# One more slot between a spectrum job's products and its way back, in a kernel of attention and a long convolution

## Chip, core and metric

The kernel runs on one core of one Trainium2 chip. The metric is the device time of one execution in microseconds (us), the median of several runs. Beside the runs there is one execution that the hardware profiler recorded; all rows of a trace come from that one.

## What is computed

Two independent layers over 2048 positions and 448 channels, float32, put side by side in the output:

```python
def _A_ref(u, log_A_real, A_imag, C_real, C_imag, log_dt, D_skip):   # a state-space convolution
    dt = jnp.exp(log_dt)
    A = -jnp.exp(log_A_real) + 1j * A_imag
    C = (C_real + 1j * C_imag) * dt[:, None]
    P = jnp.exp((A * dt[:, None])[:, :, None] * pos[None, None, :])
    K = 2.0 * jnp.einsum("dn,dnl->dl", C, P).real
    Kf, Uf = jnp.fft.rfft(K, 2 * L), jnp.fft.rfft(u_t, 2 * L)
    y = jnp.fft.irfft(Uf * Kf[None], 2 * L)[:, :, :L]
    return y + u * D_skip                                            # (transposed back)
def _B_ref(x, wqkv, wo):                                             # attention, 16 heads of 28
    q, k, v = split_heads(x @ wqkv)
    p = softmax(q @ k.T * Dh ** -0.5)
    return merge_heads(p @ v) @ wo
out = concatenate([_A_ref(...), _B_ref(...)], axis=-1)
```

## The kernel before

**The attention sets the rhythm.** After a stage of projections the kernel runs 256 steps (`NS`, line 32): 16 units `u` (4 groups of 4 heads times 4 blocks of 512 queries), with 16 blocks of 128 keys each. A step `s` does, for the current unit, four score matmuls into `pss`, each followed by an exponential on ScalarE (`s_mm`, line 714), and for the step before the four products of probabilities and values into `po` (`pv_step`, line 721, eight matmul records of 128x512). It also does, for the unit after, four matmuls into `pm` whose maxima VectorE takes (`max_mm`); these run 19 steps ahead, so they end at step 236, and the steps from 237 on are shorter. Within a step the order is written out by hand:

```python
ORDER = ('m0', 's0', 'm1', 's1', 'v', 'f', 'pv', 'f', 'v', 'k', 'm2', 's2', 'm3', 's3', 'v')
FX, PD, GAP = 1, 2, 2
```

All engines keep this program order in the stage.

**Slots.** Each `'f'` is a slot: `slot(s_)` (line 957) counts it in `n_slot` and runs at most one small task of other work, the first that is ready in this list: urgent tasks of the attention (the sums of the exponentials and the scaling of a finished unit, `fin`, line 734; the transposed maxima), an output projection (`project`, line 760), kernel powers and the input's transform, and then the convolution's spectra (kind "s"), and when none of these can run, its finish jobs (kind "f"). A step has two slots, one ahead of the `po` matmuls and one behind them; from step 238 on (`late`) a third one follows at the step's end. Behind the last step a loop calls `slot` until nothing is left.

**Spectra.** From step 195 on, 16 jobs (2 halves `f` of the channels, 8 blocks each) multiply the two transforms (`spectrum`, line 776). A job has four tasks: `forth(0)`: 16 matmul records `pm<-yk,mw`, and two VectorE products `pr` with the input's transform `ub`; `last`: `forth(1)`, the same for the other part, and then `join(0)` and `join(1)`, two GpSimd (POOL) instructions each, which make `p0` and `p1` of the products; `back(0)`: 16 matmul records `pm<-p,mw` that read `p0`, a copy `y` on ScalarE and a DMA to `z`; `back(1)`: the same from `p1`. In front of each task stands the number of slots that it must stay behind the task before it:

```python
return load, [(0, lambda: forth(0)), (0, last), (GAP, lambda: back(0)), (0, lambda: back(1))], None
```

and `f_slot` (line 929) tests it, in slots and not in time:

```python
gap, t = f_tasks[kind][0]
if n_slot[0] < f_next[kind] + gap:
    return False
```

Where a spectrum task has to wait, the slot goes to a finish job if one is ready, and stays empty otherwise. The tiles `pr` and `p` have one buffer, and the loads of the next job's `yk`, `mw` and `ub` are issued when a job's first task is taken up.

**Finish jobs.** For each half, once its 8 spectra are done (`s_done`, line 915), four jobs (`finish`, line 819) load `zi` (896 KB, from the `z` of all eight spectra) and the input `ut`, scale `ut` on GpSimd, and run four tasks of 8 matmul records `pm<-zi,wb` with an addition on VectorE into `ot` and, every second time, two DMAs to the output. A finish job starts at the earliest three steps after its load (`FL`).

All DMAs are issued in order on the SP queue. Every row of the trace bears line 75 (L75), where a helper records the instructions, so rows are told apart by their tiles.

Of the kernel before, what the change touches and what calls it, by code (L numbers as in the profile page):

```python
# [33 lines left out]
ORDER = ('m0', 's0', 'm1', 's1', 'v', 'f', 'pv', 'f', 'v', 'k', 'm2', 's2', 'm3', 's3', 'v')  # L34
PB = 8
F1 = 2
FX, PD, GAP = 1, 2, 2
FL = {"s": 2, "f": 3}
S0, SP, SW, SD, PW, E3 = 0, 4, 0, 5, 37, 8
UG = (2, 2, 4)  # L40
# [1089 lines left out]
```

## Time and profile before

| | |
|---|---|
| median of 3 runs | 1319.46 us (1316.6 to 1322.87) |
| the profiled execution | 1316.79 us, of which its instructions span 1315.1 |
| mean granted TensorE clock | 0.98 |
| busy in the span | TensorE 94%, VectorE 72%, ScalarE 72%, GpSimd 66% |

A row of the timeline has the start and the duration in us, engine, operation, the tile written and the tiles read, the shape, and how many instructions were merged; in brackets the idle time of the engine ahead of it and what ended it. PE is TensorE, DVE VectorE, ACT ScalarE, POOL GpSimd, SPq a DMA issued from SP. A row of the windows has the length of the stretch, the busy time of each engine with its count, the granted clock, the DMA share and GB/s. A row of the waits has who waited for whom, the total in us, the number of times and the longest.

### The profile page before, as it was taken

How to read it: one execution, taken by the hardware profiler on the slowest of the kernel's cores; microseconds unless marked ns; L12 is line 12 of the kernel's file. 1: busy time of each engine (PE TensorE's matmuls, PEld its weight loads, DVE VectorE, ACT ScalarE, POOL GpSimd, SP SyncE). 2: the span in 40 equal slices, each digit the busy share in tenths (PEclk: the TensorE clock that was granted, in tenths of full speed). 3: DMA queues.
4: the chain of work that ended last, by engine and by line, in shares of the span. 5: the costliest groups of instructions: out<-in, count | busy, mean ns of one | idle time of the engine just before them, and what ended most of it. 6: DMA issues, size and time to landing. Idle time of an engine off the chain costs nothing.

```text
span 1315.1 us, 33199 instructions
## 1 busy us (share of the span) xinstructions
PE 1229.7 (94%) x12625; PEld 698.8 (53%) x12625; DVE 948.6 (72%) x2106; ACT 953.0 (72%) x2068; POOL 870.4 (66%) x736
## 2 busy tenths in 40 slices
PE   6879985899999999999999999999999899999897
PEld 4657763455555555555555555555555444544333
DVE  5898887878777777778778888888887545645111
ACT  4876762488888888888788888888887656646453
POOL 3686681398887788887779999989993414423311
PEclk9989987899999999999999999999999999999999
DMA  6677769736765546468633233732416553925485
GB/s 190 206 276 260 242 205 285 220 73 143 179 147 132 129 136 175 131 174 224 167 100 87 61 78 90 161 80 70 101 37 175 178 158 132 284 87 186 132 219 137
DMA packets 200087, 205.35 MB, mean 156 GB/s; under 512 B 95992, under 2 KB 158520, under 8 KB 197880
## 3 DMA queue, kind: packets, MB, share of 16 engines
q1 hardware_dynamic: 199928, 203.23, 55.9%
q8 instruction: 100, 1.64, 0.5%
q14 instruction: 59, 0.48, 0.1%
HBM read 120.73 MB, written 82.18 MB: 154 GB/s over the span
## 4 chain that ended last, share of the span: by engine, by line
PE 71%; DVE 9%; POOL 7%; DMA 5%; ACT 4%; issue 4%; SPq 0%; ACTq 0%; POOLq 0%; DVEq 0%
PE pm L75 40%; PE pss L75 16%; PE po L75 15%; POOL p L75 2%; DMA k<-hl 2%; DVE tri L75 2%; POOL e L75 1%; DVE mx L75 1%; POOL qhat L75 1%; DVE sg L75 1%; ACT tri L75 1%; DVE px L75 1%; DVE qhat L75 1%; DMA khat<-k 1%; ACT p L75 1%
## 5 line engine op out<-in xcount | busy, mean ns | idle before, releaser
L75 ACT ACTIVATE p<-pss 128x512 f32<-128x512 f32 x1024 | 560.9, 610 | 112.3 <-PE pss L75 109.1
L75 DVE TENSOR_REDUCE mx<-pm 128x1 f32<-128x512 f32 x500 | 321.7, 684 | 125.5 <-PE pm L75 123.4
L75 PE MATMUL pss<-qhat,khat 128*128 128x512 f32 x1024 | 403.3, 400 | 2.3 <-ACT p L75 2.3
L75 PE MATMUL pm<-khat,qhat 128*128 128x512 f32 x749 | 327.1, 440 | 3.4 <-DVE mx L75 2.3
L75 POOL TENSOR_TENSOR e<-e,sdb 128x256 f32<-128x256 f32 x168 | 202.1, 1203 | 118.4 <-ACT e L75 63.1
L75 PE MATMUL po<-p,v 128*32 128x512 f32 x2048 | 269.8, 595 | 0.0
L75 POOL TENSOR_TENSOR e<-e,eu 128x256 f32<-128x256 f32 x168 | 248.3, 1478 | 13.2
L75 PEld LDWEIGHTS pm<-khat,qhat 128*128 128x128 f32 x749 | 141.9, 190 | 197.3 <-ACT p L75 41.9
L75 DVE CUSTOM_DVE_ANT_0 rl<-pm,rl 128x512 f32<-128x512 f32 x249 | 171.5, 689 | 64.8 <-ACT rl L75 61.8
L75 PEld LDWEIGHTS pss<-qhat,khat 128*128 128x128 f32 x1024 | 191.1, 189 | 49.0 <-issue 12.2
L75 POOL TENSOR_TENSOR eu<-e,sdb 128x256 f32<-128x256 f32 x168 | 202.3, 1204 | 0.0
L75 POOL TENSOR_TENSOR p<-pr,pr 64x448 f32<-64x448 f32 x64 | 73.0, 1141 | 149.6 <-PE pm L75 128.6
L75 ACT ACTIVATE rl<-pm 128x512 f32<-128x512 f32 x249 | 150.8, 606 | 20.9 <-PE pm L75 20.9
L75 DVE TENSOR_TENSOR g<-g,zg 128x128 f32<-128x128 f32 x392 | 162.1, 414 | 3.4
L75 PE MATMUL pm<-xh,khat 112*128 112x512 f32 x256 | 90.6, 436 | 21.8 <-DVE hl L75 10.5
L75 PE MATMUL pm<-kdif,qhat 128*128 128x512 f32 x249 | 101.3, 407 | 2.4 <-DMA v<-v 1.3
L75 DVE TENSOR_TENSOR zg<-g,zg 128x128 f32<-128x128 f32 x224 | 87.9, 393 | 5.0
L75 PEld LDWEIGHTS pm<-e,g 128*32 128x32 f32 x3584 | 57.2, 109 | 43.8 <-issue 17.0
L75 ACT ACTIVATE y<-pm 128x448 f32<-128x448 f32 x48 | 26.4, 549 | 73.1 <-PE pm L75 37.7
L75 PE MATMUL pm<-e,g 128*32 128x64 f32 x3584 | 73.1, 222 | 1.9 <-POOL e L75 1.9
L75 PEld LDWEIGHTS pm<-xh,khat 112*128 112x128 f32 x256 | 52.0, 208 | 37.8 <-DVE hl L75 12.9
L75 ACT ACTIVATE ub<-pm 128x224 f32<-128x224 f32 (+1 forms) x96 | 38.8, 449 | 40.0 <-PE pm L75 38.1
(134 smaller groups left out, 1468.7 us busy)
## 6 DMA issues: line engine op xcount, KB each, us to landing
sdb<-sd SPq DMA_DIRECT2D x56, 336.0 KB
khat<-k SPq DMA_DIRECT2D x64, 256.0 KB
qhat<-q SPq DMA_DIRECT2D x64, 256.0 KB
sd<-sg SPq DMA_DIRECT2D x8, 1456.0 KB
k<-hl SPq DMA_DIRECT2D x16, 512.0 KB
q<-hl SPq DMA_DIRECT2D x16, 512.0 KB
mw<-in_mw SPq DMA_DIRECT2D x16, 512.0 KB
sd<-qhat SPq DMA_DIRECT2D x8, 896.0 KB
```

The source lines that it names most:

```text
L75: i = f(*args, **kw)
```

## The change

`GAP` is 3 in place of 2: `back(0)` of a spectrum job may be issued in the third slot behind `last` at the earliest, and not in the second. Nothing else is edited. Each step is still built by the same functions, so the tasks of the spectra and the finish jobs shift against the attention's matmuls: the first job keeps its slots, the fifteen others move, the last `back(1)` stands in step 247 in place of 241, and the first finish job of the second half starts in step 250 in place of 249. Of the tasks of the finish jobs, three more run behind the last step.

```diff
-FX, PD, GAP = 1, 2, 2
+FX, PD, GAP = 1, 2, 3
```

## The prediction

> **What bounds the kernel now.** I read the page's engine line first, then busy time by stage, the waits of the stage that runs the spectra, and TensorE's timeline there.
>
> ```profile
> PE 1229.7 (94%) x12625; PEld 698.8 (53%) x12625; DVE 948.6 (72%) x2106; ACT 953.0 (72%) x2068; POOL 870.4 (66%) x736
> 900.00:950.00 50.00, 49.81 (x610) 28.40 (x610) 43.62 (x106) 42.34 (x97) 46.07 (x37) 1.00 0.34 83
> 1000.00:1050.00 50.00, 45.82 (x492) 24.82 (x492) 29.73 (x63) 31.20 (x63) 18.24 (x16) 1.00 0.51 167
> PE pm L75 <- POOL p L75: 14.4, 18, 2.0
> ```
>
> TensorE sets the pace (94%). Before the spectra (900 to 950, columns PE, PEld, DVE, ACT, POOL, clock, DMA) it stands at 49.81 of 50 us; once they run it falls to 45.82, while VectorE and ScalarE have 20 us to spare and POOL 30. So nobody else is the limit: TensorE waits, and the last row (taken over 990 to 1265) says for whom: 18 times for POOL's tile `p`, the input of the way back. One job in TensorE's timeline, with its VectorE and POOL work:
>
> ```profile
> 1092.46 0.39 PE L75 MATMUL pss<-qhat,khat 128*128 128x512 f32 x1
> 1092.78 0.96 PE L75 MATMUL pm<-p,mw 128*32 128x224 f32 x16
> 1093.56 1.04 PE L75 MATMUL po<-p,v 128*32 128x512 f32 x8
> 1094.42 0.94 PE L75 MATMUL pm<-yk,mw 128*32 128x224 f32 x16
> ...
> 1097.41 0.96 PE L75 MATMUL pm<-yk,mw 128*32 128x224 f32 x16
> 1098.19 1.04 PE L75 MATMUL po<-p,v 128*32 128x512 f32 x8
> 1099.16 0.50 PE L75 MATMUL pm<-khat,qhat 128*128 128x512 f32 x1
> ...
> 1100.89 0.39 PE L75 MATMUL pss<-qhat,khat 128*128 128x512 f32 x1
> 1102.16 0.96 PE L75 MATMUL pm<-p,mw 128*32 128x224 f32 x16 [0.88 <-POOL p L75]
> 1102.94 1.04 PE L75 MATMUL po<-p,v 128*32 128x512 f32 x8
> 1104.59 0.96 PE L75 MATMUL pm<-p,mw 128*32 128x224 f32 x16 [0.61 <-POOL p L75]
> 1098.44 1.16 DVE L75 TENSOR_TENSOR pr<-pm,ub 128x448 f32<-128x448 f32 x2
> 1099.77 4.76 POOL L75 TENSOR_TENSOR p<-pr,pr 64x448 f32<-64x448 f32 x4 [9.63 <-PE pm L75]
> ```
>
> `yk,mw` is a forth, `p,mw` a back. The second forth (in `last`) starts at 1097.41; its products end 1099.60, then POOL's four joins take 4.76 us. back(0) needs the first two of them and starts at 1102.16, 4.75 us after the forth; back(1) needs all and starts at 1104.59, 7.18 after it. These two distances are the job's own latency, and the change does not alter them. GAP 2 puts back(0) one step behind the forth, at 1100.89 + 0.32 = 1101.21 if it could, hence the wait. (A slot follows a `pss` at 0.32 us, 1092.46 to 1092.78, and a `po` at 0.86, 1093.56 to 1094.42; the bracketed idle counts from the modelled end of the matmul, 0.39 and 1.04, so it understates the delay by 0.07 or 0.18.)
>
> **What the change removes.** The row of waits holds 14.4 us in 18; with 0.13 each for the modelled ends that is 16.7. One more is hidden by a half clock:
>
> ```profile
> 1214.61 0.94 PE L75 MATMUL pm<-yk,mw 128*32 128x224 f32 x16
> 1219.30 0.96 PE L75 MATMUL pm<-p,mw 128*32 128x224 f32 x16 [1.92 <-POOL p L75]
> 1220.08 1.75 PE L75 MATMUL po<-p,v 128*32 128x512 f32 x8
> 1221.73 1.72 PE L75 MATMUL pm<-p,mw 128*32 128x224 f32 x16
> 1218.00:1221.00 3.00, 1.70 (x24) 0.68 (x24) 0.00 (x0) 0.82 (x2) 2.79 (x4) 0.88 1.07 370
> 1221.00:1224.00 3.00, 3.00 (x22) 1.02 (x18) 0.00 (x0) 0.44 (x1) 0.67 (x1) 0.55 1.05 244
> ```
>
> The back(1) at 1221.73 comes 2.43 us after its back(0), where 0.78 + 0.86 = 1.64 would do: 0.8 more. Together 17.5 us. Behind the 1.92 us wait the granted clock falls to 0.55; the 16 matmuls take 1.72 instead of 0.96 us, and with the `pss` behind them some 0.9 us are lost, which go with the wait. [...]
>
> **What is left of the waits.** I followed the slot function, and the built order of both programs, job by job. Of the 16 jobs, job 0 keeps its slots. Where the forth lies in the slot behind `pv`, or an urgent task, projection or finish task stands between, the third slot puts back(0) over 5 us behind it and back(1) in a later step: no wait (jobs 2, 3, 4, 7 to 11, 13, 14). Where the forth lies in the slot ahead of `pv` and the slots between are empty (jobs 1, 5, 6), back(0) now comes behind the next step's `pv`: 0.78 (1097.41 to 1098.19) + 0.97 (to 1099.16) + 2.05 (to 1101.21) + 0.86 = 4.66 us, against 4.75: 0.1 each, 0.3 in all; back(1) is then half a step later and free.
>
> Jobs 12 and 15 fall into the steps without maximum matmuls, which are short:
>
> ```profile
> 1270.22 0.59 PE L75 MATMUL pm<-zi,wb 128*32 128x224 f32 x8
> 1270.63 1.04 PE L75 MATMUL po<-p,v 128*32 128x512 f32 x8
> 1271.49 0.56 PE L75 MATMUL pm<-zi,wb 128*32 128x224 f32 x8
> 1271.98 0.73 PE L75 MATMUL pss<-qhat,khat 128*128 128x512 f32 x2
> 1272.64 0.59 PE L75 MATMUL pm<-zi,wb 128*32 128x224 f32 x8
> 1273.82 0.59 PE L75 MATMUL pm<-zi,wb 128*32 128x224 f32 x8
> 1276.43 0.49 PE L75 MATMUL pss<-qhat,khat 128*128 128x512 f32 x1 [0.29 <-ACT p L75]
> 1279.58 0.59 PE L75 MATMUL pm<-zi,wb 128*32 128x224 f32 x8
> ```
>
> Three filled slots make a step of 3.60 us (1270.22 to 1273.82): three finish tasks of 0.41, 0.49 and 0.52, a `pv` of 0.86 and two pairs of `pss` of 0.66. With a forth (0.78 or 0.87) in place of one finish task, three slots span 3.95 us: back(0) waits 0.8. Then back(1) is one slot on, 0.87 + 0.66 or 0.78 + 0.86 us, against 2.43: 0.85. Both jobs: 3.3. So 3.6 us of waits stay, and 17.5 - 3.6 = 13.9 go. Bounds: 17.5 if none stays, 10.3 if twice as much stays as I count.
>
> **What moves.** The work itself is the same instructions. The job that ended in step 241 ends in 247, and a few finish tasks (`zi,wb`) move later. In a step whose two later slots are empty, TensorE waits for an exponential (0.29, row 1276.43): two of them, 1273.82 to 1279.58 with one task of 0.41, take 5.76 us, 2.68 each without the task, where a filled one takes 3.60 less its three tasks, 2.18. So such a step wastes 0.5 us. Before, seven steps of these are so (245, 247, 248, 250, 251, 253, 254), after it five (249, 251, 252, 254, 255): 1.0 gained. Three finish tasks more run behind the last step:
>
> ```profile
> 1295.63 1.08 PE L75 MATMUL pm<-ident,rb 128*32 128x128 f32 x32 [1.05 <-ACT rb L75]
> 1288.93 0.59 PE L75 MATMUL pm<-zi,wb 128*32 128x224 f32 x8
> ```
>
> One of them fills part of the 1.05 us wait for `rb`: 0.4 gained. The others cost no more there than in a step.
>
> **What it adds.** The second half's finish jobs need every block `z` of that half. Before, the last back was six steps ahead of the first such load; now the load stands one slot behind it, as it does for the first half in the trace of before:
>
> ```profile
> 1116.83 0.96 PE L75 MATMUL pm<-p,mw 128*32 128x224 f32 x16
> 1118.62 0.37 SPq L75 DMA_DIRECT2D z<-y  x1
> 1121.12 0.57 SPq L75 DMA_DIRECT2D zi<-z  x1
> 1259.78 0.40 SPq L75 DMA_DIRECT2D zi<-z  x1
> 1260.28 1.34 SPq L75 DMA_DIRECT2D ut<-in_A_u  x2
> 1267.48 2.11 POOL L75 TENSOR_TENSOR ut<-ut,dsk 128x896 f32<-128x896 f32 x1 [10.38 <-DMA ut<-in_A_u]
> ```
>
> From the back (1116.83) to the load's issue (1121.12) are 4.3 us, on SP behind the `z` write; only the finish job's own loads and outputs queue behind it there. A load with its `ut` behind it has landed at most 7.7 us later (1259.78 to 1267.48), so `zi` is there between 4.3 and 12.0 us after the back. Its first matmul stands in step 250; by the slot costs above it comes 0.87 + 0.66 + 0.52 + 0.66 (rest of step 247), 3.6 (248), 2.65 (249) = 9.0 us after the back. So TensorE waits 0 to 3.0 us. `ut` was issued later and landed last, so `zi` is well below its bound: I take 0.5. [...]
>
> **Sum.** 13.9 + 0.9 + 1.0 + 0.4 - 0.5 = 15.7 us off the profiled execution's 1316.79 (span 1315.1 and 1.7 around it): 1301.1. That execution is 2.7 below the median of 1319.46, so for a median I say 1303.8, which is 1.2% less.
>
> **Rivals.**
> Another engine takes over the wait. In the stage VectorE holds the products and maxima, and could hold TensorE where POOL did; half of the 15.7 would remain: 1311.6. Against it: 29.73 of 50 us busy, and 43.62 beside a TensorE at 49.81.
> The `z` load is late: 3.0 us of wait instead of 0.5, and a half clock behind it at the 0.9 it cost above: 1303.8 + 3.4 = 1307.2. For it: a write and a read that depends on it now stand in a row. [...] Against: `zi` has `ut` behind it in the 7.7 us.
> Slower: the finish transfers become the chain that ends last. From the last back the new order leaves about 51 us to the end (9.0; two rounds of three steps, 3.60 + 5.76 each; and 23.5 from the third of the half's finish jobs on: it started at 1288.93, 26.2 before the end, and now has one filled step of 3.6 less and two tasks more behind it); the four remaining loads at 7.7 us in a row, 4.3 ahead of them and some 9 behind make 44. At twice the 7.7 they make 75, 24 us past the end: 1328. It decides from about 9.4 us a load on, and eats the whole gain at 13.4. Nothing in the trace is near that, but the loads now start later and closer together.
> That the change does nothing is out as to the order: 15 of 16 jobs shift. That its waits were covered by later slack (no change) is possible only if something other than TensorE sets the end, and the windows say no.
>
> **How the numbers follow.** Forecast 0.70, half of it 0.14, late load 0.09, slower 0.05, no change 0.02. About 0.5% (6.6 us) is what a measurement can tell here: faster means below 1312.9. A third of the half case lies above that, so faster 0.88, same 0.07, slower 0.05. The range: below, no wait left (19.8 off) and runs that scatter by 3 us, 1298; above, the half case, 1312.
>
> **What would show it.** In the profile after: the waits of TensorE for POOL's `p` between 990 and 1265 down from 14.4 to about 3, in jobs 12 and 15; TensorE at 47 or more of 50 us in each window from 1000 to 1250; the last back about 6 us later against the steps; no idle time on a `zi` load over 1 us. I am wrong if the wait moves to VectorE or to `zi`, or if the loads of `zi` are busy back to back up to the end.

## Result and profile after

The changed kernel took 1304.03 us (median of 6 runs, 1300.7 to 1307.78) against 1320.41 us before on the same chip (6 runs, 1316.6 to 1324.67): a ratio of 0.9878, 95% interval 0.985 to 0.9905. Forecast were 1303.8 us (1298 to 1312), with a chance of 0.88 that it is faster. The profiled execution took 1302.99 us, of which 1301.1 are the span, against 1316.79 and 1315.1.

First TensorE's own waits in the changed kernel between 990 and 1262 us (total, times, longest):

```profile
PE pm L75 <- POOL p L75: 2.8, 4, 0.8
PE pm L75 <- DMA zi<-z: 0.3, 1, 0.3
```

Its windows (length, then PE, PEld, DVE, ACT, POOL busy, clock, DMA share, GB/s):

```profile
900.00:950.00 50.00, 49.81 (x613) 28.52 (x609) 43.63 (x105) 42.33 (x97) 46.03 (x36) 1.00 0.34 82
1000.00:1050.00 50.00, 49.46 (x489) 27.14 (x491) 33.85 (x70) 35.15 (x71) 17.38 (x16) 1.00 0.49 163
1200.00:1250.00 50.00, 47.24 (x570) 19.86 (x570) 10.79 (x22) 24.81 (x47) 20.33 (x17) 1.00 0.54 173
```

The row of 14.4 us in 18 waits has become 2.8 in 4, and TensorE, at 45.82 of 50 us from 1000 to 1050 before, now stands at 49.46, as in the stage ahead of the spectra. Job 1 in TensorE's timeline, and the two jobs that still wait (12, and below the second "..." 15), with the first finish task of the second half and the last ones:

```profile
997.36 0.94 PE L75 MATMUL pm<-yk,mw 128*32 128x224 f32 x16
...
1018.35 0.96 PE L75 MATMUL pm<-yk,mw 128*32 128x224 f32 x16 [0.40 <-DVE mx L75]
1023.11 0.96 PE L75 MATMUL pm<-p,mw 128*32 128x224 f32 x16
1026.04 0.96 PE L75 MATMUL pm<-p,mw 128*32 128x224 f32 x16
...
1198.46 0.96 PE L75 MATMUL pm<-yk,mw 128*32 128x224 f32 x16
1203.18 0.96 PE L75 MATMUL pm<-p,mw 128*32 128x224 f32 x16 [0.67 <-POOL p L75]
1205.61 0.96 PE L75 MATMUL pm<-p,mw 128*32 128x224 f32 x16 [0.80 <-POOL p L75]
...
1241.80 0.96 PE L75 MATMUL pm<-yk,mw 128*32 128x224 f32 x16
1246.55 0.96 PE L75 MATMUL pm<-p,mw 128*32 128x224 f32 x16 [0.70 <-POOL p L75]
1248.95 0.96 PE L75 MATMUL pm<-p,mw 128*32 128x224 f32 x16 [0.58 <-POOL p L75]
...
1258.32 0.59 PE L75 MATMUL pm<-zi,wb 128*32 128x224 f32 x8 [0.28 <-DMA zi<-z]
1280.36 1.08 PE L75 MATMUL pm<-ident,rb 128*32 128x128 f32 x32 [0.68 <-ACT rb L75]
1294.41 1.32 PE L75 MATMUL pm<-zi,wb 128*32 128x224 f32 x24
```

back(0) of job 1 starts 4.76 us behind its forth and shows no wait; in jobs 12 and 15 back(0) stands 4.72 and 4.75 behind, and back(1) 7.15, which is the job's own latency again. The first finish task waits 0.28 us for its load. The stretch from the first forth to the end of the span took 303.7 us (from 997.36). Before it was 318.4 (first forth at 996.67). These 14.7 us are the change's; the spans differ by 14.0, as the profiled execution of the changed kernel was 0.7 us later at its first forth, ahead of which nothing was edited.

### The profile page after: what moved, and what is told of

Its sections match the earlier page's. It is cut to its first block, busy times and chain, and to the rows that moved or that the text cites. A ratio compares the mean times of both kernels' runs of the same rounds, so it can differ in the third digit from the quotient of the medians.

```text
span 1301.1 us, 33177 instructions
## 1 busy us (share of the span) xinstructions
PE 1228.2 (94%) x12625; PEld 701.0 (54%) x12625; DVE 948.0 (73%) x2106; ACT 952.4 (73%) x2068; POOL 871.1 (67%) x736
## 4 chain that ended last, share of the span: by engine, by line
PE 71%; DVE 10%; DMA 6%; POOL 5%; ACT 3%; issue 3%; SPq 0%; POOLq 0%; ACTq 0%; DVEq 0%
PE pm L75 40%; PE pss L75 16%; PE po L75 15%; DVE tri L75 2%; DVE mx L75 2%; POOL e L75 1%; POOL qhat L75 1%; DMA k<-hl 1%; ACT tri L75 1%; DVE qhat L75 1%; DVE sg L75 1%; DMA tri<-in_B_wqkv 1%; DVE px L75 1%; DMA khat<-k 1%; DMA ut<-in_A_u 1%
## 5 line engine op out<-in xcount | busy, mean ns | idle before, releaser
L75 PE MATMUL pm<-xh,khat 112*128 112x512 f32 x256 | 94.1, 451 | 23.2 <-DVE hl L75 11.1
L75 DVE TENSOR_TENSOR pr<-pm,ub 128x448 f32<-128x448 f32 x64 | 37.0, 619 | 56.4 <-PE pm L75 42.0
```

Source lines behind the costliest of these rows:

```text
L75: i = f(*args, **kw)
```

## Experiments

The theory (W): the third slot pays because it is longer than the latency from a job's second forth through VectorE's products and POOL's joins to the way back; TensorE's waits go, and where the other tasks come to stand is worth little. The first rival (R): the gain comes from where they stand. Stretches below are from the first forth to the end of the span in the profiled execution; they leave out the scatter of the stages ahead. The changed kernel was profiled three times and gave 303.7, 304.1 and 303.8; the others were profiled once each.

**Two slots without joins.** The joins are dropped, the order stays that of before:

```diff
-            nc.gpsimd.tensor_tensor(t_["p", e][:64], t_[0, 0][es], t_[1, 1][es], ALU.subtract)
-            nc.gpsimd.tensor_tensor(t_["p", e][64:], t_[0, 1][es], t_[1, 0][es], ALU.add)
+            t_["p", e] = t_[1, e]
```

> The kernel before (two slots), with the joins left out: the way back reads the second products as they are, so the spectra's output is not the reference's. Order of all other instructions as before. Theory W (the gain of the third slot is TensorE's waits on POOL's joins): the 17.7 us of waits and the 0.9 us of half clock behind one of them go with the joins, so about 1302 us, as much as or a little below the changed kernel. Rival R (the gain comes from where the later tasks now stand: fewer half-empty steps, finish tasks in the tail): the tasks stand where they stood, so it stays at about 1320.

Measured: 1298.73 us, 0.9848 of before (0.9831 to 0.9866).

**Three slots without joins.** The same edit on the changed kernel.

> The changed kernel (three slots), with the joins left out in the same way. Theory W: only the 3.9 us of waits that are left in the changed kernel go: about 1300 us, and within 2 us of the kernel with two slots and no joins, since where the tasks stand is worth 0 to 2 us. Rival R: about 1304 us, and some 16 us below the kernel with two slots and no joins.

Measured: 1300.14 us, 0.9854 of before (0.9838 to 0.9869). With the two kernels themselves this makes a square (stretch in us, first forths at 996.48 and 998.70, spans 1295.7 and 1298.2 in the kernels without joins):

| | joins on POOL | no joins |
|---|---|---|
| two slots | 318.4 | 299.2 |
| three slots | 303.7 | 299.5 |

With two slots the joins cost TensorE 19.2 us, with three 4.2. Without joins the third slot is worth nothing (0.3 us longer). So W is shown and R has fallen: the whole gain lies in the waits. The kernel with three slots and no joins also shows how far back(0) stands behind the forth when nothing is waited for, here in jobs 1 and 12 (`pr` is read in place of `p`):

```profile
1019.65 0.96 PE L75 MATMUL pm<-yk,mw 128*32 128x224 f32 x16 [0.40 <-DVE mx L75]
1024.33 0.94 PE L75 MATMUL pm<-pr,mw 128*32 128x224 f32 x16
...
1198.73 0.96 PE L75 MATMUL pm<-yk,mw 128*32 128x224 f32 x16
1202.71 0.96 PE L75 MATMUL pm<-pr,mw 128*32 128x224 f32 x16
1204.26 0.96 PE L75 MATMUL pm<-pr,mw 128*32 128x224 f32 x16
```

That is 4.68 us in job 1 and 3.98 in job 12, against the 4.75 that the joins need.

**Four slots.**

```diff
-FX, PD, GAP = 1, 2, 3
+FX, PD, GAP = 1, 2, 4
```

> Four slots in place of three. Theory W: the 3.9 us of waits left are gone, but the last way back stands in step 252, the first finish job of the second half in step 255, and 13 finish tasks behind the last step in place of 7, where the last load (issued when its buffer comes free) has only four tasks of 0.4 us to hide behind: some 5 us of it are bare. About 1306 us (1303 to 1310), no gain over three slots. Rival R: moving the tasks further goes on gaining: 1295 or less.

Measured: 1314.16 us, 0.9973 of before (0.9959 to 0.9988), 10 us above three slots (the stretch is 314.6 us, 10.9 above). The direction was right, the size was not, and the waits for `p` are not gone either: 1.6 us in four stay. Its timeline of TensorE:

```profile
1258.47 0.96 PE L75 MATMUL pm<-p,mw 128*32 128x224 f32 x16 [0.79 <-POOL p L75]
1269.47 0.59 PE L75 MATMUL pm<-zi,wb 128*32 128x224 f32 x8 [2.08 <-DMA zi<-z]
1271.18 1.05 PE L75 MATMUL pm<-zi,wb 128*32 128x224 f32 x8
1300.69 3.22 PE L75 MATMUL pm<-zi,wb 128*32 128x224 f32 x32 [6.93 <-DMA zi<-z]
```

and of SP, the load of the second half's first finish job, the last load and the last outputs, with the last scaling of `ut` on POOL and the last additions on VectorE:

```profile
1264.01 0.36 SPq L75 DMA_DIRECT2D zi<-z  x1
1294.55 0.55 SPq L75 DMA_DIRECT2D zi<-z  x1
1296.61 11.40 SPq L75 DMA_DIRECT2D out<-ot  x8
1302.59 2.08 POOL L75 TENSOR_TENSOR ut<-ut,dsk 128x896 f32<-128x896 f32 x1 [8.79 <-DMA ut<-in_A_u]
1304.69 1.28 DVE L75 TENSOR_TENSOR ot<-pm,ut 128x224 f32<-128x224 f32 x4 [9.58 <-POOL ut L75]
```

The load behind the last way back (1258.47, issued 1264.01) now makes TensorE wait 2.08 us, the last load 6.93 us with nothing beside it, and behind both TensorE is slower: 8 finish matmuls take 1.05 us in place of 0.59 (the granted clock is 0.94 over the window from 1250 to 1300, 0.99 with three slots), and the last 32 take 3.22 us where 24 took 1.32 above. At the very end TensorE is not what counts: its last matmuls end at 1303.91, but VectorE's last additions wait for `ut`, loaded behind the last `zi` and scaled on POOL until 1304.67, and the last outputs for them. I had counted 5 us of bare load, and neither the wait of 2.08 us, nor the slower matmuls behind the waits, nor the scaling of `ut`.

**Three slots, joins twice.** Each of a job's four POOL instructions is issued twice.

> The changed kernel with each of the four joins of a job done twice in a row (same result): the first way back is ready 7.1 us behind the forth in place of 4.75, the second 11.9 in place of 7.2. Theory W: waits of 4 to 4.5 us per job come back in the jobs with nothing of length between forth and back (about 12 of 16), TensorE's rows for POOL's p show 45 to 55 us, and the time is 1345 to 1360. Rival R: POOL has room (67% busy), so the time stays at 1304 to 1310.

Measured: 1364.43 us, 1.0343 of before (1.0326 to 1.036), 4 us above my range. Waits of TensorE (990 to 1320):

```profile
PE pm L75 <- POOL p L75: 42.1, 26, 3.1
```

and two windows:

```profile
1000.00:1050.00 50.00, 42.39 (x404) 23.37 (x400) 24.86 (x51) 27.72 (x54) 27.23 (x24) 0.90 0.36 127
1100.00:1150.00 50.00, 42.47 (x343) 23.31 (x343) 26.34 (x53) 27.92 (x55) 25.80 (x23) 0.91 0.41 136
```

POOL has 23 of 50 us to spare and TensorE waits all the same: what counts is latency, not room. The latencies are as forecast: where both wait, back(0) starts 7.1 us behind the forth and back(1) 11.9 to 12.0. The waits came out below the 45 to 55 expected, and they are not the whole time: the stretch is 59.6 us longer than with single joins (363.3 against 303.7), the waits for `p` 39.3. The rest fits the clock: in the seven windows of 50 us from 1000 to 1350 it is 0.90, 0.97, 0.91, 0.99, 0.94, 0.89 and 0.97, which makes some 21 us (an estimate: 50 us times what each lacks to 1.00).

**One slot.** `GAP` is 1.

> One slot in place of two. Theory W: from forth to second way back a job still needs 7.2 us and has some 3.8 us of slots: 3.4 us of waits in each job with nothing of length between, about 14 of them, 45 to 50 us in place of 17.7, so 1345 to 1355, though the last way back already stands in step 235. Rival R: an earlier end of the spectra is no loss: 1315 to 1325.

Measured: 1348.43 us, 1.0223 of before (1.0198 to 1.0247). The time lies in the range, but not by the forecast waits alone, which (990 to 1290) are:

```profile
PE pm L75 <- POOL p L75: 33.8, 22, 2.9
```

That is 19.4 us more than with two slots where 27 to 32 were expected; the stretch is 28.6 us longer (347.0 against 318.4). The clock is 0.93, 0.92 and 0.97 in the three windows from 1050 to 1200, which makes some 9 us (estimated as above) that I had not counted: that the time was met is in part luck. So one to four slots give 1348, about 1319, 1304 and 1314 us.

**Joins split over two engines.** If only latency against distance counts, a shorter latency does what a third slot does:

```diff
-            nc.gpsimd.tensor_tensor(t_["p", e][64:], t_[0, 1][es], t_[1, 0][es], ALU.add)
+            nc.vector.tensor_tensor(t_["p", e][64:], t_[0, 1][es], t_[1, 0][es], ALU.add)
```

With two slots:

> The kernel before (two slots), with the second instruction of each join moved from POOL to VectorE: the same slots as before, a shorter latency (first way back ready about 3.6 us behind the forth in place of 4.75, second 4.8 in place of 7.2). Theory W: what counts is the time between products and way back against their latency, not the number of slots; nearly all waits in full steps go, and some 1 us each in jobs 14 and 15 stays: about 1302 us. Rival V (VectorE, which then holds 4.5 us of work in a step with two forths, takes over the wait, or it and POOL keep each other from reading): 1308 to 1318.

Measured: 1316.29 us, 0.9986 of before (0.9973 to 0.9999). With three:

> The changed kernel (three slots) with the same split of the joins. Theory W: the 4.2 us that the joins still cost with three slots go, down to what the kernel without joins showed: about 1300 us, 3 to 4 us below the changed kernel, the fastest of all. Rival V: the same as the changed kernel or slower, 1304 to 1312.

Measured: 1308.37 us, 0.9924 of before (0.9911 to 0.9937), 3.4 us above the changed kernel on the same chip (the intervals just touch, the stretch is 308.9 against 304.1). Here W missed twice and the rival held. The joins' instructions before, from the view of the tile `p` (shortest, median and longest in ns, first and last start):

```profile
L75 POOL TENSOR_TENSOR p<-pr,pr x64: 1121/1142/1157, 1002.8 to 1232.9; 64x448 f32<-64x448 f32 x64
```

and split, with two slots:

```profile
L75 DVE TENSOR_TENSOR p<-pr,pr x32: 618/1179/1477, 1002.9 to 1228.4; 64x448 f32<-64x448 f32 x32
L75 POOL TENSOR_TENSOR p<-pr,pr x32: 1402/1444/1514, 1003.0 to 1229.4; 64x448 f32<-64x448 f32 x32
```

TensorE's waits (990 to 1290) with two slots and the split:

```profile
PE pm L75 <- DVE mx L75: 4.0, 7, 2.0
PE pm L75 <- POOL p L75: 3.7, 5, 1.5
PE pm L75 <- ACT rl L75: 2.1, 5, 0.8
PE pm L75 <- DVE ot L75: 2.0, 2, 1.0
```

and with three:

```profile
PE pm L75 <- DVE mx L75: 3.7, 6, 2.0
PE pm L75 <- ACT rl L75: 2.4, 6, 0.8
```

The two engines hold each other up: POOL's instructions take 1.40 to 1.51 us in place of 1.14, and on VectorE the first of a job's two takes 0.62 us (once 0.92) and the second 1.44 to 1.48; the median of 1.18 lies between the two groups. The four instructions of a job end in turn, see the last section. And TensorE now waits for the maxima that stand behind the joins on VectorE, where that row had 0.4 us before, and for two tiles that had no row at all: `rl`, which ScalarE makes for the maxima, and `ot`. With two slots 10.7 us of waits for `p` went, as W said, and 7.7 came back in these three rows; the stretch is only 2.5 us shorter (315.9 against 318.4). The wait changed its owner. With three slots the 2.8 for `p` went and 5.7 came; why TensorE waits for `rl` I did not follow up.

**The changed kernel again**, on that chip:

> The changed kernel once more, on the chip of the two splits, to compare with them: 1304 us.

Measured: 1305.01 us, 0.9898 of before (0.9883 to 0.9914).

**Split only where VectorE is free.** From step 238 on there are no maxima:

```diff
+            (nc.vector if late[0] else nc.gpsimd).tensor_tensor(t_["p", e][64:], ...
```

> The changed kernel with the join's second instruction on VectorE only from step 238 on (jobs 12 to 15), where no maxima are left for VectorE to take. Theory (the split lost because TensorE then waited for maxima behind the joins, and because VectorE and POOL slow each other): there is nothing behind the joins here, the first way back is ready some 3.8 us behind the forth (4.75 with POOL alone), the second some 5.3 (7.2), so the 3.3 us of waits of jobs 12 and 15 go: 3 us below the changed kernel on the same chip, about 1301. Rival (the slow-down of the two engines alone eats it): no difference, 1304.

> The changed kernel once more, on the same chip beside the late split, to compare with it: 1304 us, and 2.8 us of TensorE's waits for POOL's p.

Measured: 1298.99 us, 0.9859 of before (0.9839 to 0.988), against 1302.90 us, 0.9883 (0.9863 to 0.9902), for the changed kernel beside it. The intervals overlap; the stretch is 300.7 us against 303.8, and the row of waits for POOL's `p` (2.7 us in the kernel beside it) is gone. The stretch is 3.1 us shorter where 3.3 were expected. By its median it is the fastest kernel with the whole computation.

## Why the prediction was right

**The waits.** Forecast were 17.5 us of waits before and 3.6 after, 13.9 gone, by laying the slots of the built order against two distances from the trace, 4.75 and 7.18 us. After the change the waits stand where they were put: jobs 12 and 15, two each, 2.8 us by the row and 3.3 with 0.13 for each modelled end. 17.5 less 3.3 are 14.2. The square gives it without the rows of waits: 19.2 less 4.2, 15.0, with the half clock in it. The lengths behind the sum hold too: without joins back(0) stands 4.68 to 4.69 us behind the forth in jobs 1, 5 and 6 (forecast 4.66) and 3.98 in jobs 12 and 15 (forecast 3.95). One reading of the order was wrong: jobs 2, 7 and 8, which I had put at over 5 us and so clear of any wait, stand at 4.69, 4.69 and 4.95 there, and at 4.76, 4.90 and 4.93 in the changed kernel. It cost at most 0.2 us a job, but that it was so little is luck. And one sign was written wrongly: the last back comes six steps later, which is 14.0 us (1234.95 before, 1248.95 after) and not about 6.

**The half clock.** 0.9 us were to go with it. In the windows from 1000 to 1250 the clock is now 1.00, where before it was 0.97 from 1200 to 1250. That such a drop can come with waits is seen in three other kernels: with one slot (waits for `p` of up to 2.9 us) the clock is 0.93 and 0.92 in the two windows from 1050 to 1150, with four (2.08 us for `zi`) 0.94 from 1250 to 1300, with joins twice (up to 3.1 us) 0.89 to 0.99 from 1000 to 1350.

**What moves** is the term that was mis-sized. I had +1.0 for fewer half-empty steps, +0.4 for the wait for `rb`, -0.5 for the `z` load: 0.9 us of gain, and the square shows 0.3 of loss. `rb` is as forecast (the wait fell from 1.05 to 0.68), the load cost 0.28 (forecast 0.5, bounds 0 to 3.0), and the half-empty steps did get fewer: TensorE's waits for ScalarE's `p` fell from 2.3 us in eight to 1.4 in five. Missing is the end: three finish tasks instead of one stand behind the last projection, and two more output DMAs. From the last one's start to the end of the span it was 5.4 us (1309.69 to 1315.1), now 5.9 (1294.41 + 0.76 to 1301.1). With these 0.5 us and the 0.2 that the load was better, some 0.9 us of the loss stay that I could not assign.

**The sum.** Forecast 15.7 us off; the stretch shows 14.7. The medians show 16.4, 12.7 and 15.6 on the three occasions (1304.03, 1305.01 and 1302.90 against 1320.41, 1317.73 and 1318.52): the median adds the scatter of both kernels, so that 1304.03 is only 0.2 us from the forecast is partly luck.

**The rivals.** The late load and the finish transfers at the end did not decide with three slots and did with four, so the place was right. The 9.4 us a load from which I had them decide held for three slots and was not tested; with four the first load is used 5.5 us after its issue (1264.01 to 1269.47) and the last 6.1 (1294.55 to 1300.69), with too little work beside them. VectorE taking over the wait did not happen either; in part it does as soon as VectorE gets half of the joins.

## What to carry over

A hand-written order that counts slots hides a time; to choose the count, measure the latency of the chain that has to fit in and lay it against the slots' length where the work is densest and where it is thinnest. One slot too few costs its shortfall in every job that has no other long work in between; one too many cost here only where the end became bare, so look at the tail before going further. Where a stage has an engine with nothing queued behind it, shorten the chain there instead of waiting longer.

## What the runs showed of the hardware

The granted TensorE clock fell behind a wait of TensorE of 1.92 us in the kernel before: it is 0.55 in the window from 1221 to 1224 that follows. In the kernel with joins twice, with 26 waits of up to 3.1 us between 990 and 1320, it is 0.90 over the 50 us from 1000; there 16 matmuls of a way back took 1.72 us right behind a wait of 3.08 (1247.72) and 0.96 behind one of 2.27 (1027.60). Not every wait of about 2 us did it: behind the wait of 2.04 us in job 15 of the kernel before (back(0) at 1231.66) the clock stayed at 1.00 (window from 1230 to 1236).

And the joins on VectorE and POOL, each with two inputs from the tiles `pr`, ended in turn. These are the four instructions of one job's joins in the late split, two on VectorE and two on POOL:

```profile
1199.32 0.62 DVE L75 TENSOR_TENSOR p<-pr,pr 64x448 f32<-64x448 f32 x1
1199.97 1.45 DVE L75 TENSOR_TENSOR p<-pr,pr 64x448 f32<-64x448 f32 x1
1199.43 1.50 POOL L75 TENSOR_TENSOR p<-pr,pr 64x448 f32<-64x448 f32 x1 [1.18 <-DVE pr L75]
1201.01 1.42 POOL L75 TENSOR_TENSOR p<-pr,pr 64x448 f32<-64x448 f32 x1
```

They end at 1199.94 (VectorE), 1200.93 (POOL), 1201.42 (VectorE) and 1202.43 (POOL). The first takes 0.62 us although POOL's starts 0.11 us behind it, and each of the others ends 1.0 (POOL) or 0.5 us (VectorE) behind the one before it, however early it started. Together they take 3.1 us; with POOL alone the four took 4.76, 1.14 each. Full times in turn would be 3.5 us (twice 0.62 and twice 1.14; no join ran alone on VectorE, so its 0.62 is the first one's). The 0.4 less are 0.13 for each of the three that ended behind another (both are estimates from these rows and the 1.14 of POOL alone). The same order and the same 3.1 us (1023.92 to 1027.04 in one with two slots, 1025.98 to 1029.11 in one with three) stand in every job of the two full splits, but for one of 3.4 whose first join met a scaling of `ut` on POOL.
